# Where a chunk's normalised activations are transposed: TensorE and ScalarE in place of VectorE and DRAM, in a kernel with a written-out instruction order

## The chip, the cores and the metric

One core of a Trainium2 chip runs the whole kernel. The metric is device time in microseconds, the median of several executions. Engines: TensorE (PE, with its weight loads PEld), VectorE (DVE), ScalarE (ACT), GpSimd (POOL), and SyncE (SP), which here only issues DMAs.

## What is computed

A gated linear-attention recurrence over 768 steps, then one layer-norm and two-layer MLP with a residual.

```python
# q, k, v, alpha: (batch 4, heads 8, seq 768, dim 48), float32
for t in range(S):
    state = alpha[:, :, t, :, None] * state + einsum('bhd,bhe->bhde', k[:, :, t], v[:, :, t])
    y[:, :, t] = einsum('bhd,bhde->bhe', q[:, :, t], state)
x = y.transpose(0, 2, 1, 3).reshape(B, S, H * D)           # (4, 768, 384)
xn = (x - mean(x)) / sqrt(var(x) + 1e-6) * g_ln
out = x + maximum(xn @ w_ch1, 0) @ w_ch2                   # w_ch1 384 x 1536, w_ch2 1536 x 384
```

The two weights come as 64-bit floats; the kernel turns them into 32-bit ones itself.

## The kernel before

The sequence is cut into 6 chunks of 128 steps (c = 0 to 5). With 4 batches that makes 24 attention steps, each written as a Python generator (`attention`), which yields after every few instructions. Its stages: the logarithm of alpha and its running sum on PE (`lps`), two exponentials, the scaled q and k (L323, L325), their transposes (`kT`, `qT`: on PE for chunks 0 and 1, L351, and with VectorE's 32 x 32 transposes and a round trip over DRAM, `tr` and `td`, from chunk 2 on, L362 to L377), the scores (`aps`, L393 or L401), the causal mask (L407, L413), the state update (`sums`, L428, L437 to L443), the outputs (`yps`, L454 or L459 and L463), and the layer norm to `xn` (L466 to L515). The plain `x` goes to DRAM (`kept`) and comes back later as the residual (`ob`, L545).

Then `xn` (128 steps x 384) must be turned so that the 384 lie on the partitions (`xT`). There are two ways, chosen by `c < X_BY_DMA` at L519. In the first, PE makes three transposes into one PSUM bank (`xps`, L522) and VectorE (chunk 0) or ScalarE (later chunks) copies them out (L524). In the second, VectorE transposes in 32 x 32 blocks (`xr`, L528), SP issues four stores of 48 KB (`xd`, L532) and one load that puts the blocks in their places (L535). Before, chunks 0 to 3 take the first way and chunks 4 and 5 the second.

The MLP of chunk 0 runs straight (`hidden`, L558; `project`, L570). Chunks 1 to 5 use a scheme with fewer multiplications: a matrix product of 3 x 3 by 3 x 2 blocks is made of 15 products of sums of blocks (`hidden_product`, L848, in two halves r), and the second layer of 20 products (`product`, L674). The sums of weight blocks are made once on VectorE (`combine_first`, L800; `combine_weights`, L634), those of x and of the hidden values per chunk (`combine_x`, L825; `combine_hidden`, L661). Each product's result is added to the right places by VectorE, ScalarE and POOL (L690 to L740, L856 to L891), and the hidden values pass a Relu (L898). The weights arrive in 12 pieces and are rounded by VectorE and ScalarE (L215 to L232).

PSUM has 8 banks here: two for `sums`, and six that everything else shares (`tag="bank"`). Each engine runs its instructions in the order in which they were issued; an instruction that waits holds up what is behind it on its engine. The order is not left to a scheduler. It is a string of some 1,500 letters, `ORDER`; each letter takes the generator of that name one step further. Lower-case letters a to x are the 24 attention steps (c = 4 is q to t, c = 5 is u to x), A to L the weight pieces, Y and Z the first layer of chunk 0, P and Q its second layer, S and W the weight sums, X and N the sums of x and of hidden values, 1 and 2 the hidden products, R and U the Relus, M the second products, and O the residual loads.

Of the kernel before, what the change touches and what calls it, by code (L numbers as in the profile page):

```python
# [18 lines left out]
EPS = 1e-6  # L19
STAGED = 3  # L20
BY_DMA = 2
X_BY_DMA = 4
SPLIT = 4
AHEAD = 2
G = 32
# [5 lines left out]


ORDER = (
    "bacabcadaacbcaadbcadabcababbebaccbadbaaBbccaedcbceAeeaaacbfecfBcdafddeaedbdeafae"
    "bcdccbfgadhAdcgCcdbebeebfhggdfgbfffbCdcgfgecdfchgdfhgabcddchdhAiiegjhacehedhhjfg"
    "biAdfidAeBhBijffYYiCjZZYYifZYlZCgjYDlYYjjZZYBZYgDieEgDgDjZZekEhZYGZgZigZGeeYgYgg"
    "fZYEhfGfkChihiYFYijfgEhgkhFZYhgYfghijgkFeZZlGZShfZYHlhHfYFYZeZHelYiZgllPmZkJIgJk"
    "PeiYjJIflHeSZIQgkIlYSjiPkffennSQlOKjLSnSjmSQhKnSjLnKPkiljnhSQnLkkjkWknkShOmPhkhl"
    "kOOhWlmmphmQmkmXjWQnXjlSQjPmkilXSXkP2OXWjXQjkjW2iXoSWX2oWX22Pi2mnol1j1mom2omSpoo"
    "l1XSpk2oW2m112p1m2pm11m1W211pp12O122r22jnn21lpnmnjSml1riOn2l12Rl111kqS1m21W1Rkp2"  # L40
    "o21mUXpq1mU2rUrnmj1rl2Rno2oomqonrormpokO1rNM2Mipin1op1ionoqUM2qp2W12RkMmNqiMoRtk"
    "UrpkqNM1NoMliMlNUMMNMNMKNqMlNorMWrnmtltNRMsqppMWNMriMMMpNlsqqqnoqttNttMtMsXMMssM"
    "sMNMNMX1oXXppMvstM2MXMMNMsppXoMXoqMsMMXM1nqqv11Xq1trMq2tqX21rn12v1r2ur2r222rvsqs"
    "svsu1rs1nuvvt2s11ss11p22rtsvosn2uropuXru222221uts212stnU1211u1121222Op1Rp2tRU21R"
    "Us1pXqU11x2tO2MM1vwMUM12xuRvu1vurNNNNwtOuuMwRxvNtxRNutwwMM2MOwNXwMNuXMMtNM1rMMMw"
    "qtXMMMxNUNxtMMsNMMMxXxMtXtrMMqMNrMXNvutMMwNuMMMNMMMxMLMOM11vvuq2X2O2wMus1wX11222"
    "2r2Xt1222w22utsqxvw2x2ww1vx21sX12121xwvq2O2x2w111u1uvU121w12s1wuRvx12U11J1q21R1U"
    "OvRxU121wMMu2xxsRNMw2NNMRM1MUNN2MMuUMqXN1MrNNRMNvMXNXMMMM2MMMxNM1uNXMMNMNMOXMXMv"
    "MMXOMMMXxNxwxMMvNMMMMMXMx21w1x222212v12w222x122w2212X11UX2212121121121wx111MU11X"
    "2RR2v1211212211R1URU211XOUM2XNRX1MX1RM2MXN2MXNXNMXXMXMMMN111U1MN1M1122MNM1MM2MM1"  # L50
    "11NNN121O11NM1MM21N1112N1122M1MMM12MM12N222M22M2RM1M2N22MM2MU1ON2M22M2UURR22RNNM"
    "MNM1MMOMRMNMUUM2ONMNNNMO2MMMUMNMMMMMRMMNNMMMNMNMMNMMMMMMMMNMNMMMMMMM"
)


# [1 line left out]
def kernel(  # L57
# [236 lines left out]
    def attention(c, b):  # L294
# [222 lines left out]
        if c not in xT_of:  # L517
            xT_of[c] = work.tile([P, NF, B, P], FP32, name="xT", tag="xT")
        if c < X_BY_DMA:  # L519
            xps = ps.tile([P, NF, P], FP32, name="xps", tag="bank", bufs=6)  # L520
# [439 lines left out]
```

## Time and profile before

| | us |
|---|---|
| median of 3 runs | 421.02 (420.24 to 422.59) |
| the profiled execution | 420.14 |
| its span, first to last instruction | 418.3 |
| last matmul ends (from the span's start) | 415.15 |

The page's chain of work that ended last gives 89% of the span to PE, 4% to VectorE, 2% to DMA. Its costliest lines:

```profile
PE 89%; DVE 4%; DMA 2%; ACT 2%; issue 1%; POOL 0%; POOLq 0%; SPq 0%; DVEq 0%
PE hps L848 31%; PE ops L674 30%; PE ops L570 8%; PE hps L558 7%; PE aps L401 3%; PE yps L459 2%; PE yps L463 2%; PE sums L428 2%; DMA vn<-in_v_dram 2%; PE xps L522 1%; PE aps L393 1%; DMA ra<-in_alpha_dram 1%; PE lps L313 1%; DVE w L217 1%; PE tps L351 1%
```

The hidden products and the second products are 61% of the chain; `xps` is 1%. An fp32 matmul stands in the trace as two PE instructions, a transpose as one. A group's mean duration on PE is from start to modelled end; matmuls overlap, so what one costs on the path is read from start to start.

### The profile page before, as it was taken

To read this page: it belongs to the slowest core of one execution; us is meant where nothing else is said; L and a number is where in the kernel's file an instruction comes from. 1 tells how busy PE (TensorE), PEld (TensorE's weight loads), DVE (VectorE), ACT (ScalarE), POOL (GpSimd) and SP (SyncE) were. 2 spreads that over 40 slices of the span, in tenths; PEclk is the share of its full clock that TensorE was granted. 3 is DMA by queue.
4 is the path that set the end of the run, shared out by engine and by line. 5 is a ranking of instruction groups with operands and counts; after the bars stand their busy time and mean duration, and the time that the engine had idled before them with its cause. 6 is when DMAs were issued, how large, how long until landed. Compare 5 with 4: busy or idle time off the path is not lost.

```text
span 418.3 us, 11560 instructions
## 1 busy us (share of the span) xinstructions
PE 409.8 (98%) x4608; PEld 361.3 (86%) x4608; DVE 351.4 (84%) x713; ACT 177.5 (42%) x440; POOL 151.6 (36%) x164
## 2 busy tenths in 40 slices
PE   7998999999999999999999999999999999999996
PEld 5787888766578889998889999889998899999996
DVE  4999999999999989996888995688876767977873
ACT  5598447724243496414546603364313242014110
POOL 1011000003203980043395033493152940499123
PEclk9999999999999999999999999999999999999999
DMA  8999999987888778587684546433035200001201
GB/s 278 340 302 288 235 196 306 270 184 195 193 233 175 207 153 193 123 203 179 135 213 85 130 102 162 88 96 78 0 116 102 67 0 2 1 19 40 94 20 56
DMA packets 135037, 61.26 MB, mean 146 GB/s; under 512 B 90908, under 2 KB 131100, under 8 KB 134984
## 3 DMA queue, kind: packets, MB, share of 16 engines
q1 hardware_dynamic: 134440, 60.37, 56.1%
q8 instruction: 36, 0.59, 0.6%
q10 hardware_dynamic: 544, 0.17, 0.2%
q14 instruction: 17, 0.14, 0.1%
HBM read 43.12 MB, written 17.39 MB: 145 GB/s over the span
## 4 chain that ended last, share of the span: by engine, by line
PE 89%; DVE 4%; DMA 2%; ACT 2%; issue 1%; POOL 0%; POOLq 0%; SPq 0%; DVEq 0%
PE hps L848 31%; PE ops L674 30%; PE ops L570 8%; PE hps L558 7%; PE aps L401 3%; PE yps L459 2%; PE yps L463 2%; PE sums L428 2%; DMA vn<-in_v_dram 2%; PE xps L522 1%; PE aps L393 1%; DMA ra<-in_alpha_dram 1%; PE lps L313 1%; DVE w L217 1%; PE tps L351 1%
## 5 line engine op out<-in xcount | busy, mean ns | idle before, releaser
L690 POOL TENSOR_TENSOR ob<-ob,u 128x192 f32<-128x192 f32 x40 | 26.2, 665 | 64.5 <-DVE ob L687 48.3
L848 PE MATMUL hps<-sum,w 128*128 128x256 f32 x192 | 46.3, 381 | 0.0
L898 ACT ACTIVATE hT<-hT 128x512 f32<-128x512 f32 x48 | 28.7, 622 | 35.0 <-POOL hT L870 18.5
L443 POOL TENSOR_TENSOR mid<-mid,gate 112x192 f32<-112x192 f32 x20 | 11.6, 580 | 81.8 <-DVE mid L441 51.3
L674 PE MATMUL ops<-w,hT 128*128 128x192 f32 x224 | 40.5, 327 | 0.0
L848 PEld LDWEIGHTS hps<-sum,w 128*128 128x128 f32 x192 | 36.1, 190 | 5.0
L674 PEld LDWEIGHTS ops<-w,hT 128*128 128x128 f32 x224 | 37.1, 190 | 0.7 <-issue 0.2
L848 PE MATMUL hps<-xT,w 128*128 128x256 f32 x136 | 34.0, 380 | 0.0
L570 PE MATMUL ops<-w,hT 128*128 128x384 f32 x96 | 33.0, 492 | 0.0
L558 PE MATMUL hps<-xT,w 128*128 128x256 f32 x144 | 32.5, 382 | 0.0
L558 PEld LDWEIGHTS hps<-xT,w 128*128 128x128 f32 x144 | 27.0, 190 | 4.2
L674 PE MATMUL ops<-ws,sum 128*128 128x192 f32 x160 | 28.7, 327 | 0.0
L848 PEld LDWEIGHTS hps<-xT,w 128*128 128x128 f32 x136 | 25.5, 190 | 3.1
L570 PEld LDWEIGHTS ops<-w,hT 128*128 128x128 f32 x96 | 17.5, 190 | 10.8 <-DVE w L232 0.4
L674 PEld LDWEIGHTS ops<-ws,sum 128*128 128x128 f32 x160 | 26.5, 190 | 0.3
L684 DVE TENSOR_TENSOR ob<-ops,ob 128x192 f32<-128x192 f32 x50 | 17.2, 351 | 10.6 <-PE ops L674 6.5
L443 POOL TENSOR_TENSOR st<-st,gate 112x192 f32<-112x192 f32 x16 | 11.6, 725 | 35.6 <-DVE st L441 25.9
L674 PE MATMUL ops<-ws,hT 128*128 128x192 f32 x128 | 23.6, 328 | 0.0
L459 PEld LDWEIGHTS yps<-st,qT 48*64 48x64 f32 x320 | 19.9, 134 | 4.0 <-issue 2.3
L463 PE MATMUL yps<-vx,at 64*64 64x48 f32 x320 | 22.7, 219 | 0.0
L401 PEld LDWEIGHTS aps<-qT,kT 48*64 48x64 f32 x576 | 19.1, 134 | 4.1 <-issue 0.8
L459 PE MATMUL yps<-st,qT 48*64 48x48 f32 x320 | 22.0, 220 | 0.6 <-ACT x L486 0.6
(248 smaller groups left out, 1131.6 us busy)
## 6 DMA issues: line engine op xcount, KB each, us to landing
ws<-in_moe_w_ch_dram SPq DMA_DIRECT2D x12, 768.0 KB, 5.8
td<-tr SPq DMA_DIRECT2D x64, 96.0 KB, 2.8
vn<-in_v_dram SPq DMA_DIRECT2D x12, 384.0 KB, 6.9
kept<-x SPq DMA_DIRECT2D x24, 192.0 KB, 3.0
ob<-kept SPq DMA_DIRECT2D x24, 192.0 KB, 3.0
out_dram<-ob SPq DMA_DIRECT2D x19, 192.0 KB, 1.9
ra<-in_alpha_dram SPq DMA_DIRECT2D x16, 192.0 KB, 2.6
kT<-td SPq DMA_DIRECT2D x32, 96.0 KB, 3.4
```

Source lines behind the costliest of these rows:

```text
L401: nc.tensor.matmul(to, kT[rs, p, s], qT[rs, p, s], start=True, stop=True)
L428: nc.tensor.matmul(up[h, p], qk_of(c, b)[ts, 1, p, i, :h.stop - h.start], vn[ts, i, p], start=True, stop=True)
L443: nc.gpsimd.tensor_mul(new, new, by)
L459: nc.tensor.matmul(yps[i][halves[s], i, p], qT[rs, p, s], (now, mid)[s][rs, p], start=True, stop=r != i)
L463: nc.tensor.matmul(yps[r][halves[s], i, p], at[halves[r], p, s], by, start=r != i, stop=True)
L558: nc.tensor.matmul(hps, w1[:, j // 2, f, j % 2 * P:][:, :P], xT_of[0][:, f, bs], start=(f == 0), stop=(f == NF - 1))
L570: nc.tensor.matmul(ops_of[b], hT_of[c][:, j, b], w2[:, j], start=(j == 0), stop=(j == NJ - 1))
L674: nc.tensor.matmul(acc, lhs[:, j], rhs[:, j], start=(j == 0), stop=(j == NT - 1))
L684: nc.vector.tensor_add(x, acc, x)
L690: getattr(nc.gpsimd, f"tensor_{op}")(x, x, y)
L848: nc.tensor.matmul(acc[:, i], w, b, start=True, stop=True)
L898: nc.scalar.activation(out=x, in_=x, func=AFT.Relu)
```

## The change

One number and the string. Chunk 4 (attention steps q, r, s, t) now takes the first way at L519: three TensorE transposes and a ScalarE copy for each of its four batches, in place of one VectorE transpose, four stores and a load. Chunk 5 stays on the second way. These four steps have one yield less each, so the string has four letters less (1504 for 1508), and all of it was searched anew, so that nearly every engine's instructions stand in another order, from the first attention steps to the last products.

```diff
-X_BY_DMA = 4
+X_BY_DMA = 5
...
 ORDER = (
-    "bacabcadaacbcaadbcadabcababbebaccbadbaaBbccaedcbceAeeaaacbfecfBcdafddeaedbdeafae"
-    "bcdccbfgadhAdcgCcdbebeebfhggdfgbfffbCdcgfgecdfchgdfhgabcddchdhAiiegjhacehedhhjfg"
...
+    "abacabccadbbcacdbababbbbadaaaaccbadacbcecbaBccfaedeAeaaacefaecbfbcddddfbdeaafdcB"
+    "bdeaegdaceAchCbechbeeadcdgcbfcgcfbfgfcdfcgdbdddgCfehgfghhhbdegehdAibegdchefhigfd"
...
-    "11NNN121O11NM1MM21N1112N1122M1MMM12MM12N222M22M2RM1M2N22MM2MU1ON2M22M2UURR22RNNM"
-    "MNM1MMOMRMNMUUM2ONMNNNMO2MMMUMNMMMMMRMMNNMMMNMNMMNMMMMMMMMNMNMMMMMMM"
+    "M1MNMN1XM12MR11M1M1NM111M222R2M22MMMMMMNMN12N222MM2M2M2MM11U222RM222UMRUOMOMMMM2"
+    "ONMNN2MURUO22NMMNNMNUMMMNMMMMMMRMMMNNNMMMMNNMNMMMMMNMNMMMMMMMMMM"
```

More of the change, by code (lines that the diff above doesn't have):

```diff
@@ L33 @@
 ORDER = (
-    "bacabcadaacbcaadbcadabcababbebaccbadbaaBbccaedcbceAeeaaacbfecfBcdafddeaedbdeafae"
-    "bcdccbfgadhAdcgCcdbebeebfhggdfgbfffbCdcgfgecdfchgdfhgabcddchdhAiiegjhacehedhhjfg"
[L36 to L50, printed above, removed]
-    "11NNN121O11NM1MM21N1112N1122M1MMM12MM12N222M22M2RM1M2N22MM2MU1ON2M22M2UURR22RNNM"
@@ L52 @@
-    "MNM1MMOMRMNMUUM2ONMNNNMO2MMMUMNMMMMMRMMNNMMMNMNMMNMMMMMMMMNMNMMMMMMM"
+    "abacabccadbbcacdbababbbbadaaaaccbadacbcecbaBccfaedeAeaaacefaecbfbcddddfbdeaafdcB"
+    "bdeaegdaceAchCbechbeeadcdgcbfcgcfbfgfcdfcgdbdddgCfehgfghhhbdegehdAibegdchefhigfd"
+    "jjhhAAZgaBiBZjCBjijgZZiifYZiCYZifZYfDjegYeYlgejgDZYDYkYDYEZZlZYjgZfghhEGYfhgCZge"
+    "GEigYFfYZZYjhfhGkgYZijFZYZFYESYYkfYHhgiYHZlkfFigifgjhHZGleShgYShlZQeikefllklgZfn"
+    "YhSgJSjIHJQOIJekIflnfZPKeYekPSSQKOiiKZSljmjIQhlPnknjSnSnLLPnjOLkmSkknhOikkhShkkm"
@@ new lines @@
+    "WPjhllQmmmhmSWmPkhXQXWXnWPijXjQmiXSXjoX1S11lOP12l1op2QWXkmiSko2lW1jWmX2o2oooo2qW"
+    "2X22pmWmn12jqpSpl1p11j2p1m2pm12122pr22mmji2Okr1n211Ojninmlk1m2n21R21knU2lX1211Rl"
+    "U2W2pUm11npjr1krolpooRoUrnmonMnojrkor1irok221o1MplRnWiqpqRqoqqmUoNM1MNMMMqNNMkpi"
+    "1lMrNpRM2ltMNiolMpWMOs2qniMMpNmktlMopNroNMrWMrNUMNlqtMNnqqqsttoqtMqttMvJsMMMNNLM"
+    "MsmXossMMMMpmNNsqvmMpoMXMMXtMMmsMq1MnMqqXrtX2XXr11121r22X2Xq221ts12X2pvvv1u11r1p"
+    "rrs21ssuspsvpp1vuqt2srs2r2t1vOsuutu2s12t1121R2x12ouXnouO2r2x1r1tun112O1Uw2RnnR22"
@@ new lines @@
+    "p1Usw222UMpsMM11qM22tMv1Nut2UMN1UONuuRRNtMtNXwMMMUtXNwNsvuvxNM1wXNMxRtxNsx1MMxs2"
+    "MNqrMNMMMMMuMMwMuMNwNrMMxvMvuMXXMMwMXMNMMqqNMxXMuMMvu21X11r21v22Xus2212u12wsu1M2"
+    "22X21wO1wwxwv2x2Owq21w1uOt21x211qrrX1t222u122vUwx12Uxv1wwxs1t2112RROU1112x2RMMUM"
+    "sw1NMRt112tXxNNUXMXNRXv1KMMM1MNMMMwNMXNNRNx2NMMvUuMNxwMMXxMMMxuM12MvMNvNXxOMMMNv"
+    "MMMvNwNMMMMMxwMMMXXM2x1112vxw112Mx1111w1XX112O211222122211221122R1222122U1O2w21U"
+    "122vXR1RU1uR222MMM21X1MU1XMNX2N1RXXXNXMUMXM1O2NMX12NN12NMU1M11122111RN111N211NM1"
```

## The prediction

> **What bounds the kernel now.** I read the page's busy line first, then the same busy times by stretches, then what TensorE (PE) waited for, then the chain of waits, then single groups and the stretch around two tight places.
>
> ```profile
> PE 409.8 (98%) x4608; PEld 361.3 (86%) x4608; DVE 351.4 (84%) x713; ACT 177.5 (42%) x440; POOL 151.6 (36%) x164
> ```
>
> A share over the whole span hides where an engine is the limit, so the stretches come next. Columns: the stretch, its length, then busy time and (instructions) of PE, PE's weight loads, VectorE (DVE), ScalarE (ACT) and GpSimd (POOL), granted clock, DMA share, GB/s.
>
> ```profile
> 0.00:38.76 38.76, 34.10 (x573) 27.99 (x573) 32.13 (x71) 28.08 (x72) 5.12 (x10) 1.00 0.97 303
> 38.76:115.00 76.24, 75.57 (x972) 57.01 (x968) 74.43 (x132) 37.16 (x89) 10.53 (x13) 1.00 0.90 228
> 115.00:200.00 85.00, 84.93 (x1330) 75.76 (x1333) 77.04 (x161) 41.47 (x109) 33.27 (x37) 1.00 0.76 183
> 200.00:300.00 100.00, 100.00 (x1123) 91.71 (x1116) 82.98 (x186) 46.48 (x123) 45.97 (x46) 1.00 0.49 111
> 300.00:410.00 110.00, 110.00 (x603) 104.01 (x602) 81.86 (x159) 24.04 (x49) 53.88 (x53) 1.00 0.16 44
> ```
>
> The first hidden matmul starts at 38.76. From there PE has 0.74 us without work up to 410, and its clock is granted in full: this is a PE-bound kernel after the start. Up to 115 us VectorE is as full (74.43 of 76.24): there the two bind together. Chunk 4's x, which the change moves, is worked on between 244 and 292 us, where PE has no idle time at all and VectorE has about a sixth.
>
> ```profile
> PE lps L313 <- ACT la L308: 1.6, 2, 1.4
> PE xps L522 <- DVE xn L511: 1.5, 1, 1.5
> PE yps L459 <- ACT x L486: 0.6, 1, 0.6
> ```
>
> Columns: us in total, times, longest. The first two are of the start (before 34 us); the third is the only one left later, at 114 us. PE never waits for x's way over DRAM (xr, xd). So shortening that way can't shorten the run, and work given to PE adds to it.
>
> **The change, part by part.** The rows (line, engine, operation, count, busy us, mean ns):
>
> ```profile
> L522 PE MATMUL xps<-consts,xn 128*128 128x128 f32 x48 | 7.8, 278 | 1.5 <-DVE xn L511 1.5
> L528 DVE STREAM_TRANSPOSE xr<-xn 128x384 f32<-128x384 f32 x8 | 4.5, 568 | 0.0
> L524 ACT COPY xT<-xps 128x384 f32<-128x384 f32 x12 | 5.4, 471 | 6.8 <-PE xps L522 6.8
> ```
>
> Added: for chunk 4's 4 batches, 3 TensorE transposes and one ScalarE copy each (48 transposes become 60, 12 copies become 16). The mean of 278 ns is not the price: matmuls overlap, and the chain of waits shows what three take on the path.
>
> ```profile
> 160.89 0.33 PE xps L522 x3
> 161.22 1.30 PE ops L674 x8
> 162.52 0.33 PE xps L522 x3
> ...
> 167.80 0.48 PE xps L522 x3
> ```
>
> 0.33 us between matmuls, 0.48 right behind the small attention matmuls. Chunk 4's four groups now stand among hidden products and second products (none behind attention matmuls), so 4 x 0.33 = 1.3 us, at most 4 x 0.48 = 1.9. With no idle time on PE in that stretch all of it is path: +1.3. The Trainium skill ("TensorE: Matmul & The Clock Gate", Wait — 56ns, not 53.3ns?) has 55.6 ns from start to start of matmuls 128 wide, by which 12 would cost 0.7 us as an estimate and the sum below be 1.2; the rows here have 0.33 / 3 = 110 ns for these fp32 transposes, so the measurement decides.
>
> The 4 copies (4 x 0.47 = 1.9 us) lie on ScalarE, busy 46.48 of 100 us there: cover enough; what their waits hold up is a rival below.
>
> Removed: 4 VectorE transposes (4 x 0.57 = 2.3 us), and on SP's queue 16 stores xd and 4 loads xT. VectorE has idle time from 200 us on and PE waits for none of these: worth 0. SP's later issues (kept, gate, ob) come a little earlier; PE's waits name none of them.
>
> Moved: the order of nearly everything. I counted both programs by engine. The work ahead of PE's first hidden matmul is the same set on PE (64 transposes of q and k, 12 of x, 72 of scores and running sums, and so on) and on VectorE the same 69 rows' work, so only waits can move that point. Two places differ.
>
> First, the start. VectorE is the chain from about 8 to 38 us. Before, it does a product of the second pair of batches between the first two q/k products and the copies out of PE:
>
> ```profile
> 9.94 0.56 DVE L323 TENSOR_TENSOR qk<-rk,lps 128x384 f32<-128x384 f32 x1
> 10.55 0.69 DVE L356 COPY kT<-tps 112x512 f32<-112x512 f32 x1
> 11.16 0.55 DVE L325 TENSOR_TENSOR qk<-rq,more 128x384 f32<-128x384 f32 x1
> 11.63 0.68 DVE L356 COPY kT<-tps 112x512 f32<-112x512 f32 x1
> ```
>
> After, both copies stand ahead of these products. The 16 transposes that they read run from 9.48 to 11.39, so the second copy can end no sooner than 11.39 + 0.69 = 12.1, against 12.3 before, and two products (2 x 0.46 us from start to start) are still owed: 0.7 us later. VectorE's next waits (0.42 us for the next transposes at 15.7, 0.26 at 18.0) can swallow nearly all of that. Bounds 0 to 0.7; I take 0.35.
>
> Second, the last piece of w2. PE's projection of chunk 0 starts on it in the same nanosecond as VectorE finishes it:
>
> ```profile
> 101.96 0.96 DVE L232 SCALAR_TENSOR_TENSOR w<-w,ws 128x768 f32<-128x768 f32 x1
> 102.92 2.23 PEld L570 LDWEIGHTS ops<-w,hT 128*128 128x128 f32 x8
> ```
>
> In the new order VectorE has 12 instead of 11 of the weight sums of L800 ahead of that piece and otherwise the same, while PE's work up to there is equal: one L800 of 128x512 is 0.70 us (its group's mean 703 ns, 0.62 from start to start), so PE starts about 0.65 us later, unless VectorE's idle time is cut: between 38.76 and 115 it has 76.24 - 74.43 = 1.8 us. Bounds -1.2 (all of it gone) to +0.65. The first w2 pieces get more room, and for every product of chunks 1 to 5 I compared VectorE's summed work up to the sum that it reads with PE's summed work up to it: the smallest margin goes from 0.2 to about 0.6 us, so no new wait there, with a margin too thin to be sure. For idle time regained at all these places I take -0.4.
>
> Sum: 1.3 + 0.35 + 0.65 - 0.4 = +1.9 us. The end is alike (17 second products in a row before, 18 after; 3.2 us from the last matmul's end at 415.15 to the span's end). The profiled execution took 420.14 us (span 418.3 and 1.8 around it), 0.9 under the median of 421.02; 420.14 + 1.9 = 422.0, and the same on the median gives **422.9 us**, +0.45%.
>
> **The rivals.** (1) ScalarE's queue becomes a wait. In the new order two copies L524 stand one behind the other, of transposes that lie 8 hidden-product matmuls apart on PE (8 x 0.43 = 3.5 us), and behind them the copy out (L474) of an attention output that PE had finished before both. ScalarE works in order, so this output's two PSUM banks of six stay taken some 3.9 us longer, with the transposes' own bank besides; the next products then have three banks and their own ScalarE copies (L856, L864) queue behind. Price: up to 3.5 us of PE's time if nothing else can be issued, so 422.9 + 3.5 = 426.4. For it: the wait at 114 us is of just this kind (PE behind L486, 0.6 us, when four banks are out). Against: ScalarE is half idle, and three banks rotate. It decides from about one product's delay (0.9 us) on.
>
> (2) Not slower: the new order takes up VectorE's 1.8 us of idle time before 115 us and the 0.6 us wait at 114. Then 1.3 - 1.2 - 0.6 = -0.5: 420.5. For it: VectorE is full there and nothing on PE forces its waits. To be faster by 0.5% it would have to regain 3.4 us, more than all PE idle time after the start.
>
> (3) The path of chunk 4's x did bind, and VectorE with it: then 2.3 us come off and 1.3 go on, 420.0. The Trainium skill ("VectorE: DVE Perf Modes", Rules for kernel authors) says so: a 128x128 transpose belongs on TensorE where PSUM can take it, and plain strided DMAs are a trap. Against: 110.00 busy of 110.00 on PE, and the first hidden product of chunk 4 starts at 295.6 without a wait.
>
> **How the numbers follow.** Half a per cent (2.1 us) is about what a measurement of this kernel can tell from no change, since the three runs spread over 2.35 us. Chances: my forecast's mechanism 0.52, centred on 422.9, where its terms can vary by 1.5 us either way (half of it below the 423.1 that is +0.5%); rival 1 0.25, nearly all slower; rival 2 0.16 and rival 3 0.07, with a third of these faster by over 0.5%. So slower 0.26 + 0.22 = 0.48, faster 0.07, same 0.45. The range goes from rival 2's 420.5 to rival 1's 426.4, rounded to 420.4 and 426.4; the forecast's own is 421.4 to 424.4.
>
> **What would show it.** Right: PE busy time up by about 1.3 us; L522 x60 with 0.33 us per three on the chain between 260 and 285 us; the first hidden matmul at 38.8 to 39.5 us; the last piece of w2 at 103.3 to 104; PE idle only at the same places. Wrong: PE idle between 260 and 300 us released by ScalarE (rival 1), a first hidden matmul before 38.3 us or the third wait gone (rival 2), or a run shorter although PE does more (rival 3). A stall of PE over 1 us anywhere from 40 to 410 us that I don't name would make the sum wrong.

## The result and the profile after

The changed kernel took 425.32 us (median of 6 runs, 424.45 to 427.22) against 420.69 for before on the same chip (6 runs, 420.12 to 422.59). The ratio is 1.011, with a 95% interval of 1.0084 to 1.0135: slower by 4.6 us, where 1.9 were forecast. The profiled execution took 425.47 us and its span is 423.7, 5.4 more than before's.

The busy line of the page after, and from the groups of lines the three that the change touches (mean ns of one after the comma, then the idle time before them):

```profile
PE 413.3 (98%) x4620; PEld 362.5 (86%) x4620; DVE 352.6 (83%) x709; ACT 180.6 (43%) x444; POOL 148.5 (35%) x164
L522 PE MATMUL xps<-consts,xn 128*128 128x128 f32 x60 | 10.0, 276 | 0.5 <-DVE xn L511 0.5
L524 ACT COPY xT<-xps 128x384 f32<-128x384 f32 x16 | 7.5, 467 | 11.1 <-PE xps L522 11.1
L528 DVE STREAM_TRANSPOSE xr<-xn 128x384 f32<-128x384 f32 x4 | 2.2, 558 | 0.0
```

The change does what it says: 12 transposes more on TensorE, 4 copies more on ScalarE, 4 transposes fewer on VectorE. PE's busy time rose by 3.5 us, far more than the 1.3 us that the forecast gives 12 transposes.

The same stretches as before, except that the first one ends at 40.00, where the first hidden matmul now starts (38.8 before):

```profile
0.00:40.00 40.00, 34.53 (x572) 27.91 (x572) 32.07 (x70) 27.95 (x72) 5.48 (x10) 1.00 0.90 288
40.00:115.00 75.00, 74.87 (x915) 56.28 (x912) 73.36 (x129) 35.54 (x85) 7.04 (x12) 1.00 0.93 233
115.00:200.00 85.00, 83.53 (x1293) 73.98 (x1286) 75.85 (x158) 41.12 (x105) 31.98 (x37) 1.00 0.74 179
200.00:300.00 100.00, 99.80 (x1200) 90.69 (x1199) 80.96 (x175) 45.47 (x116) 47.35 (x47) 1.00 0.41 97
300.00:410.00 110.00, 110.00 (x599) 103.43 (x598) 84.28 (x168) 30.21 (x66) 49.93 (x49) 1.00 0.17 46
```

PE's idle time up to 115 us has shrunk (0.13 of 75.00, against 0.67 of 76.24). New is the third stretch: 1.47 us idle between 115 and 200 us, where before had 0.07. From the first hidden matmul to the end of the span it is 383.7 us now (423.7 - 40.0) and was 379.5 (418.3 - 38.8). That makes 1.2 us lost at the start and 4.2 behind it. Of the 4.2, 1.3 are the added transposes. PE's idle time explains only another 1.1 (1.80 from 40 to 410 us, against 0.74), so the rest must lie in time that counts as busy. That the modelled ends of matmuls cover short stalls is my reading of this; no view shows it directly. The distance between two fixed events is the safer measure, and the table below uses it.

What PE itself waited for (us in total, times, longest):

```profile
PE aps L401 <- ACT kT L356: 1.9, 1, 1.9
...
PE hps L848 <- ACT x L486: 0.5, 1, 0.5
PE hps L848 <- DVE u L885: 0.5, 2, 0.3
...
PE ops L674 <- ACT x L486: 0.4, 1, 0.4
```

The releaser is now ScalarE: once at the start (L356) and twice later by L486, the copy of an attention output out of PSUM. The wait for L486 that before had at 114 us is gone. What ScalarE did at the two later places (start, duration, in brackets the idle time ahead and what ended it):

```profile
142.45 1.15 ACT L898 ACTIVATE hT<-hT 128x512 f32<-128x512 f32 x2 [2.18 <-POOL hT L870]
143.51 0.47 ACT L486 ACTIVATE x<-yps 128x384 f32<-128x384 f32 x1
...
178.67 0.52 ACT L308 ACTIVATE la<-ra 128x384 f32<-128x384 f32 x1 [3.12 <-DMA ra<-in_alpha_dram]
...
180.71 0.47 ACT L486 ACTIVATE x<-yps 128x384 f32<-128x384 f32 x1
```

Both times ScalarE stands still, for GpSimd or for a load, at an instruction that PE does not need yet, and the copy that gives PE two PSUM banks back is behind it in the queue. Neither stall is long (0.53 us without work at 143 us, 0.42 at 181): no stall over 1 us stands in this trace between 40 and 410 us. The stall at the start is of the same kind. The chain of waits there, in order of time (start, duration, what):

```profile
9.38 5.94 DMA row<-eq
...
15.33 2.19 DMA gate<-row
...
18.79 6.68 DMA ra<-in_alpha_dram
...
25.49 0.52 ACT la L308
26.02 0.48 ACT kT L356
```

A 2 KB store (`row`) is issued behind the three chunk 1 loads and takes 5.94 us. The load that reads it back waits for it on SP's queue, so the later alpha load is issued at 18.79 (17.20 before), and ScalarE's logarithm waits for that with the copy of kT, which PE needs, behind it.

### The profile page after: what moved, and what is told of

Read it like the earlier page. It is cut to its first block, busy times and chain, and to the rows that moved or that the text cites. A ratio compares the mean times of both kernels' runs of the same rounds, so it can differ in the third digit from the quotient of the medians.

```text
span 423.7 us, 11548 instructions
## 1 busy us (share of the span) xinstructions
PE 413.3 (98%) x4620; PEld 362.5 (86%) x4620; DVE 352.6 (83%) x709; ACT 180.6 (43%) x444; POOL 148.5 (35%) x164
## 4 chain that ended last, share of the span: by engine, by line
PE 86%; DMA 6%; DVE 3%; ACT 2%; issue 1%; POOL 1%; SPq 0%; DVEq 0%
PE ops L674 30%; PE hps L848 29%; PE hps L558 8%; PE ops L570 7%; PE aps L401 3%; DMA ra<-in_alpha_dram 3%; PE yps L459 2%; PE yps L463 2%; PE sums L428 2%; DMA row<-eq 1%; PE xps L522 1%; DMA vn<-in_v_dram 1%; PE lps L403 1%; POOL hT L870 1%; PE tps L351 1%
## 5 line engine op out<-in xcount | busy, mean ns | idle before, releaser
L690 POOL TENSOR_TENSOR ob<-ob,u 128x192 f32<-128x192 f32 x40 | 27.5, 697 | 61.6 <-DVE ob L687 47.6
L570 PEld LDWEIGHTS ops<-w,hT 128*128 128x128 f32 x96 | 17.8, 190 | 10.7
L401 PEld LDWEIGHTS aps<-qT,kT 48*64 48x64 f32 x576 | 19.1, 134 | 5.7 <-issue 2.6
L401 PE MATMUL aps<-qT,kT 48*64 48x64 f32 x576 | 22.0, 222 | 2.0 <-ACT kT L356 1.9
L463 PE MATMUL yps<-vn,at 64*64 64x48 f32 x320 | 22.1, 220 | 0.0
```

The costliest lines, as they stand in the source:

```text
L401: nc.tensor.matmul(to, kT[rs, p, s], qT[rs, p, s], start=True, stop=True)
L463: nc.tensor.matmul(yps[r][halves[s], i, p], at[halves[r], p, s], by, start=r != i, stop=True)
L570: nc.tensor.matmul(ops_of[b], hT_of[c][:, j, b], w2[:, j], start=(j == 0), stop=(j == NJ - 1))
L690: getattr(nc.gpsimd, f"tensor_{op}")(x, x, y)
```

## The experiments

All were timed beside runs of before on the same chip. "Rest" is the span less the start of the first hidden matmul, in the profiled execution, which is one execution and not always a typical one (2.2 us above the median in x4_new_order, 2.3 in x3_store_near). The string of before is the old order, that of the changed kernel the new one. "x3", "x4", "x5", "x6" say how many chunks are transposed on TensorE.

| kernel | median us | before, same chip | ratio, 95% | first hidden matmul | rest |
|---|---|---|---|---|---|
| before | 420.69 | | | 38.8 | 379.5 |
| the changed kernel | 425.32 | 420.69 | 1.0084 to 1.0135 | 40.0 | 383.7 |
| x5_old_order | 427.00 | 420.62 | 1.0123 to 1.0171 | 38.8 | 386.1 |
| x4_new_order | 430.17 | 420.62 | 1.0203 to 1.0260 | 40.1 | 390.5 |
| x5_old_copy_near | 421.64 | 420.42 | 1.0011 to 1.0049 | 38.6 | 380.6 |
| x6_new_order | 427.13 | 420.42 | 1.0131 to 1.0210 | 39.8 | 384.5 |
| new_row_first | 424.67 | 420.62 | 1.0066 to 1.0113 | 39.6 | 383.2 |
| new_v1_later | 426.34 | 420.62 | 1.0109 to 1.0165 | 41.0 | 383.1 |
| new_copy_first | 424.24 | 420.42 | 1.0059 to 1.0109 | 39.6 | 382.1 |
| new_four_moves | 423.48 | 420.42 | 1.0042 to 1.0094 | 39.4 | 383.1 |
| new_two_moves | 422.77 | 420.68 | 1.0041 to 1.0083 | 38.9 | 383.7 |
| new_three_moves | 423.08 | 421.15 | 1.0038 to 1.0064 | 38.8 | 382.0 |
| x4_row_late | 423.32 | 420.97 | 1.0042 to 1.0090 | 41.7 | 379.3 |
| x3_old | 430.93 | 420.68 | 1.0222 to 1.0262 | 39.7 | 388.3 |
| x3_mno_old | 428.21 | 420.68 | 1.0160 to 1.0210 | 39.1 | 387.2 |
| x3_store_near | 431.42 | 421.15 | 1.0227 to 1.0261 | 40.2 | 391.7 |
| x3_mno_store_near | 429.47 | 421.15 | 1.0190 to 1.0240 | 39.9 | 387.8 |
| x3_mn | 425.11 | 420.97 | 1.0073 to 1.0120 | 39.6 | 384.2 |

**The number and the string apart.** The change has two halves, so each was run with the other's old value.

```diff
# x5_old_order: before with
-X_BY_DMA = 4
+X_BY_DMA = 5
# x4_new_order: the changed kernel with
-X_BY_DMA = 5
+X_BY_DMA = 4
# and one letter more for each of q, r, s, t, behind its 27th
```

> The order string of before, with chunk 4's x on TensorE and ScalarE (each of the four steps then does nothing at its last letter). Theory A (the transposes cost 0.33 us per three on PE, the rest of the loss comes from the new order): 420.7 + 1.3 = 422.0 us, ratio 1.003, L522 x60. Theory B (the transposes and copies of chunk 4 themselves make the loss, through banks and ScalarE's queue): near 425.3, ratio 1.011.

> The new order string, with chunk 4's x on VectorE and DRAM as before (each of the four steps gets its missing letter behind its last one). Theory A: 425.3 - 1.3 = 424.0 us, ratio 1.008 to before. Theory B: near 420.7. If chunk 4's load now lands too late for its sums, up to 2 us more than A.

By the medians both are worse than the changed kernel. In x4_new_order chunk 4's x lands too late for an order that was made for the short way. PE's waits, and the VectorE instruction behind the longest:

```profile
PE ops L674 <- DVE ob L684: 4.5, 1, 4.5
PE ops L674 <- ACT x L486: 2.2, 1, 2.2
```

```profile
298.25 0.43 DVE L825 TENSOR_TENSOR sum<-xT 128x256 f32<-128x256 f32 x1 [5.34 <-DMA xT<-xd]
```

A sum of x blocks waits 5.34 us for the load, and VectorE's next work on PE's results stands behind it. The second wait, 2.2 us for L486, is the one at 178 us again. Behind the 4.5 us stall PE's granted clock stands at 0.50 from 302.5 to 305.5 us (PE has 10 instructions from 303 to 305.5, and 17 from 306 to 308.5 at a clock of 1.00), by estimate another 1.2 us, and all six executions have a mean clock of 0.991 to 0.996, where before has 1.000 or 0.999. So neither half can be priced with the other's order. A fair price of the transposes needs an order that suits them, with nothing else moved.

**What spoils x5_old_order, and the price of the transposes.** In x5_old_order the copy stands where the stores to DRAM stood, 31 to 49 letters behind the transposes. Its transposes and copies for chunk 4 (min/median/max ns, then first and last start):

```profile
L522 PE MATMUL xps<-consts,xn x12: 272/273/329, 245.2 to 278.1; 128*128 128x128 f32 x12
...
L524 ACT COPY xT<-xps x4: 459/471/493, 263.0 to 284.2; 128x384 f32<-128x384 f32 x4
...
248.00:264.00 16.00, 12.83 (x92) 10.35 (x92) 5.81 (x18) 3.99 (x11) 3.90 (x7) 1.00 0.48 126
```

The first transposes are at 245.2 and the first copy only at 263.0: banks stay taken for 18 us, and PE is busy for 12.83 of the 16 us between. The next kernel moves the four copies alone.

```diff
# x5_old_copy_near: x5_old_order with the copy letters of q, r, s, t
-  31 to 49 letters behind their transposes
+  7 or 8 letters behind their transposes
```

> The order of before with chunk 4's x on TensorE, as in x5_old_order, but each of the four copies that free the bank stands 6 letters behind its transposes instead of 29 to 49. Theory (the transposes cost their 1.3 us of TensorE, and what x5_old_order lost beyond that were banks held too long): the five stalls of 0.6 to 1 us between 248 and 258 us are gone, time 420.6 + 1.3 = 421.9 (421.4 to 422.6), below the changed kernel's 425.3. Rival (ScalarE's added copies themselves are late, whatever the order): stalls stay, 424.5 or more. Rival (the transposes are free, because TensorE is not the bound there): 420.6.

```profile
L522 PE MATMUL xps<-consts,xn x12: 272/273/328, 244.7 to 272.4; 128*128 128x128 f32 x12
...
L524 ACT COPY xT<-xps x4: 478/479/488, 245.2 to 272.7; 128x384 f32<-128x384 f32 x4
...
248.00:264.00 16.00, 16.00 (x123) 14.44 (x123) 9.05 (x23) 5.61 (x14) 3.59 (x7) 1.00 0.53 138
```

The same views of this kernel: each copy follows at once, PE is busy for all 16 us, and the time is 421.64 instead of 427.00 with the same instructions. This is chunk 4 on TensorE with hardly anything else moved, and it costs 0.3% (0.1 to 0.5%), 1.3 us with an interval of 0.5 to 2.1; the rest of its span is 1.1 us longer than before's. The term for the transposes agrees with this. If they cost the same in the new order, the changed kernel's other 3.3 us belong to that order.

**A second dose.**

```diff
# x6_new_order: the changed kernel with
-X_BY_DMA = 5
+X_BY_DMA = 6
```

> The changed kernel with chunk 5's x on TensorE and ScalarE as well; no letter is moved (the third x letter of chunk 5 does nothing). A second dose of the same change, without a new order. Theory (the dose costs TensorE's 12 transposes, 1.3 us, and the rest of the change's loss is the order's): 425.3 + 1.3 = 426.6 (426.0 to 427.2). Rival (each dose costs the whole 4.6 us, by ScalarE or by banks): 429 to 430. Rival (chunk 5's way over DRAM binds): below 425.3.

427.13, 1.8 us above the changed kernel by the medians. The intervals of the two overlap, so the size is loose, but a dose that costs the whole 4.6 us is not what this shows. Three of its six executions have a mean granted clock of 0.995 or 0.996 (427.0 to 431.2 us), the three others took 426.1 to 427.3. The waits of the new order (ScalarE's L356 at the start, L486 at 143 us) are there again unchanged.

**The waits of the new order, one by one.** The edits move single letters (a7 is the seventh a of the string, counted from 1):

```diff
# new_row_first: the row store (a7) ahead of the chunk 1 loads (b6)
-  c d b a b a b b b b
+  c d b a a b b b b b
# new_copy_first: the copy L486 (l19) ahead of the two Relus at 142 us
-  n 2 1 R 2 1 k n U 2 l X
+  n 2 1 l R 2 1 k n U 2 X
# new_v1_later: the chunk 5 logarithm (v1) behind the copy p19
-  t t M v J s ... M M M M p m N N
+  t t M J s ... M M M M p v m N N
# new_four_moves: these three, and the chunk 1 logarithm (g1) behind the copy of kT (e10)
-  b d e a e g d a c e A c h
+  b d e a e d a c e g A c h
# new_two_moves: new_row_first and new_copy_first
# new_three_moves: new_two_moves and new_v1_later
```

> The changed kernel with two neighbouring letters swapped, so that SP issues the 2 KB store row of batch 0 (chunk 0) ahead of the three loads of chunk 1 instead of behind them. Theory A1 (that store lands late behind 1.2 MB of loads, the gate load that needs it holds SP for 3.5 us, so weights and chunk 1's second alpha come late, ScalarE waits 3.0 us for alpha and PE 2.1 us behind it): SP's stop at 12 us shrinks below 1.5 us, the first hidden matmul starts near 38.8 instead of 40.0, total 0.5 to 1.3 us less: 424.0 to 424.8. Rival: the wait moves to the next transfer and the total stays within 0.3 us.

> The changed kernel with one letter moved: the logarithm of chunk 5's batch 1 (L308) behind the copy L486 of chunk 3's batch 3 on ScalarE instead of ahead of it. Theory A2 (ScalarE waits 3.1 us for that alpha at 178 us and holds two PSUM banks behind it, PE waits 0.6 us at 180): PE's wait at 180 us goes, total 0.5 us less. Rival (VectorE or the other drains are late too): the wait stays or moves by a product, total unchanged.

> The changed kernel with the single move at 142 us: the copy that frees two PSUM banks stands ahead of the two Relus that wait 2.2 us for GpSimd. Theory (the wait in ScalarE's queue makes TensorE's stall of 0.70 us at 143 us and the lost time stays): 425.3 - 0.7 to -1.4 = 424.2. Rival (it is regained by the next wait anyway): 425.3.

> The changed kernel with four moves of letters that the profile names: the row store ahead of the chunk 1 loads (a7 before b6), the logarithm that waits 3.0 us for its load behind the copy of kT (g1 after e10), the copy out of PSUM ahead of the two Relus that wait for GpSimd at 142 us (l19 before the sixteenth-letter pair R1), and the chunk 5 logarithm that waits 3.1 us at 178 us behind the copy p19. Theory (the loss beyond 1.3 us is in these waits of the new order): -0.65 (measured for the first move alone), -0.7 to -1.4 at 143 us, -0.5 to -1.0 at 180 us, 0 to -0.5 for the second at the start: 425.3 - 2.5 = 422.8 (421.9 to 423.7). Rival (a wait that is taken away comes back later, since the same operands have to pass): 424.7, as with the first move alone.

> The changed kernel with the two moves that helped alone: the row store ahead of the chunk 1 loads (424.67 alone) and the copy ahead of the Relus at 142 us (424.24 alone); the changed kernel has 425.32. Theory (both losses are separate and stay lost): -0.65 and -1.1 add up, 423.6 (423.1 to 424.1), and the stall of 1.1 us that new_four_moves has at 151 us, which comes from moving the two logarithms, is not there. Rival (they overlap): 424.2 or more.

> new_two_moves (422.77) and the chunk 5 logarithm behind the copy p19 as well: it waits 3.1 us for its load, and TensorE stands 1.82 us at 178 us in the profile of new_two_moves. Theory (the loss of the changed kernel is the transposes and three waits of its order): 422.8 - 1.0 to -1.8 = 421.6 (421.0 to 422.2), which is before plus the 1.3 us of the transposes, within what is measured. Rival (something else of the new order costs as well, the wait comes back later): 422.5 or more.

new_copy_first came as the theory said: 424.24. ScalarE's queue there, to be compared with the stall above:

```profile
140.54 0.49 ACT L486 ACTIVATE x<-yps 128x384 f32<-128x384 f32 x1 [0.59 <-PE yps L459]
142.14 1.15 ACT L898 ACTIVATE hT<-hT 128x512 f32<-128x512 f32 x2 [1.11 <-POOL hT L870]
```

The copy now runs at 140.54 rather than 143.51, the Relus wait for GpSimd as before, PE has no wait for L486 left, and the rest of the span is 1.6 us shorter. new_row_first came to 424.67. The interval of each of the two overlaps with the changed kernel's, so the sizes of the single moves (1.1 and 0.65 us) are loose. SP's gate load, which waits for the row store, in the changed kernel and in new_two_moves, which has the same move:

```profile
12.18 3.53 SPq L419 DMA_DIRECT2D gate<-row  x2
```

```profile
12.28 0.92 SPq L419 DMA_DIRECT2D gate<-row  x2
```

The two issues take 0.92 instead of 3.53 us. In all five profiles with the new order's start they take 3.4 to 3.5 us and the first hidden matmul is at 39.6 to 41.0; with the store moved they take 0.9 to 1.4 us and it is at 38.8 to 39.6 (four profiles). Both moves together took off 2.5 us by the medians (2.0 by the ratios, whose intervals just part), down to 422.77.

new_v1_later is a miss: the stall at 180 us is gone from its trace, but the time, 426.34, is no better, and its start came 1 us later with the same instructions. The clock has a part in that start. The page's row of the granted clock (40 slices of 10.6 us, in tenths):

```profile
PEclk9989999999999999999999999999999999999999
```

Behind the 2.0 us wait for kT at 25 us the clock stands at 0.50 from 28.6 to 32.0 us, with PE busy throughout: by estimate, at half the clock, 1.7 us. In the changed kernel nearly the same wait (1.9 us) is followed by a clock of 1.00. Four of new_v1_later's six executions have a mean clock of 0.995 or 0.996 and none of the changed kernel's has; but the other two took 426.0 and 426.7, so the clock alone does not make the miss. Nor did new_three_moves better new_two_moves: the ratios, 1.0051 and 1.0062, are not to be told apart. That this wait holds PE is seen in the profile of new_two_moves, on ScalarE and on PE:

```profile
177.61 0.53 ACT L308 ACTIVATE la<-ra 128x384 f32<-128x384 f32 x1 [4.41 <-DMA ra<-in_alpha_dram]
```

```profile
PE ops L674 <- ACT x L486: 1.7, 1, 1.7
```

The logarithm waits 4.41 us for its load there, 3.12 in the changed kernel and 2.34 in new_row_first, so the price of this place differs from one execution to the next. The profiled execution of new_two_moves took 424.39, which is 1.6 above its median. new_four_moves, with g1 moved besides, was no better than new_two_moves: its trace has a new PE stall of 0.9 us at 151 us, whose cause stays open.

**The start's trait alone, in the kernel before.**

```diff
# x4_row_late: before, with b4, b5, c6 and b6 drawn ahead of a7
-  a a d b c a d a b c a b
+  a d b c d b c b a a a a
```

> Before, with nothing of the change but one trait of the new order at the start: batch 0's row store of chunk 0 stands behind the three chunk 1 loads (b6 ahead of a7, the letters b4, b5 and c6 drawn ahead with it), as in the changed kernel. The x of chunk 4 keeps its way over DRAM. Theory (a small store issued behind three large loads lands late, SP waits for it at the gate load, and the chunk 1 loads and the logarithm behind them come late): SP waits 3 to 4 us at the gate load and the first hidden product starts 0.5 to 1.3 us later, 420.7 + 0.65 = 421.3 (420.9 to 422.2). Rival (the late start comes from something else of the new order): 420.6.

423.32, more than either theory gave. The rest of the span, 379.3, is before's to 0.2 us, so the whole loss is in the start: the first hidden matmul is at 41.7. What SP's queue waited for in the first 22 us (us in total, times, longest):

```profile
SPq L419 <- DMA row<-eq: 3.9, 1, 3.9
SPq L330 <- ACT eq L320: 2.2, 1, 2.2
```

The wait at the gate load for the row store is there as foretold, 3.9 us against 1.7 in before and 4.1 in the changed kernel. But the test is less clean than meant: with the letters drawn ahead VectorE's products shift too, both row stores start later (the first at 9.15, against 7.25 before), and PE waits 1.4 us for a product (`PE tps L351 <- DVE qk L325`). So the mechanism is shown, and the size for the store alone is better read from new_row_first.

**The other direction.** If a transpose costs PE 0.11 us, before would gain by giving up more of them.

```diff
# x3_old: before, with chunk 3's x over DRAM; loads placed 16 to 22 letters behind the stores, X23 later
-X_BY_DMA = 4
+X_BY_DMA = 3
# x3_mno_old: as x3_old, the last batch left on TensorE, X23 not moved
-        if c < X_BY_DMA:
+        if c < 3 or (c, b) == (3, 3):
# x3_store_near, x3_mno_store_near: the same two, stores 6 letters behind VectorE's transposes
# x3_mn: only batches 0 and 1 of chunk 3 over DRAM, stores near
+        if c < 3 or (c == 3 and b > 1):
```

> The change turned the other way: the order of before with chunk 3's x too over VectorE's transposes and DRAM (X_BY_DMA = 3), so that TensorE transposes 36 blocks instead of 48. Its four loads of xT stand 16 to 20 letters behind their stores, and the first combining letter of chunk 3's x (X23) is moved some 50 letters back, behind the last of these loads. Theory (a transpose on TensorE costs its 0.11 us wherever TensorE is the bound, and VectorE and the DMA queues have room): 420.5 - 1.3 = 419.2 (418.7 to 420.0). Rival (chunk 3's data comes too late over DRAM, as chunk 4's did in x4_new_order): 422 or more. Rival (VectorE's four added transposes of 0.57 us bind): 421 to 423.

> As x3_old, but the last batch of chunk 3 stays on TensorE, and no combining letter is moved: nine transposes fewer than before. Theory: 420.5 - 1.0 = 419.5 (419.0 to 420.2). Rival (late data or VectorE): 421 or more.

> x3_old again (chunk 3's x over DRAM too, 12 transposes fewer than before), with the stores to DRAM 6 letters behind VectorE's transposes instead of 11 to 44, so that the buffer of the transposed row comes free early. In x3_old and x3_mno_old VectorE's next such transpose waits 6.2 us for this buffer, and TensorE 4.3 to 4.5 us for what stands behind it on VectorE. Theory (this wait was the loss there, a transpose costs TensorE 0.11 us): 420.6 - 1.3 = 419.3 (418.8 to 420.0). Rival (the way over DRAM is too late for chunk 3 whatever the order, at its last batch above all): 422 or more.

> As x3_store_near, with the last batch of chunk 3 left on TensorE and no combining letter moved. Theory: 420.6 - 1.0 = 419.6 (419.0 to 420.2). Rival: 421 or more.

> Only batches 0 and 1 of chunk 3 go over DRAM besides chunks 4 and 5 (six transposes fewer than before), stores 6 letters behind VectorE's transposes. In x3_mno_store_near two such transposes stood next to each other and the second waited 6.3 us for the row buffer of the first, whose stores waited in SP's queue. Theory (that wait was the loss, and it needs two of them together): no stall at 211 us, 420.7 - 0.65 = 420.0 (419.6 to 420.9). Rival (one such transpose alone loses as much as it saves, for it holds a row buffer until its four stores have landed): 421 to 423.

All five are misses: 425.11 to 431.42. The waits of x3_mno_store_near between 205 and 218 us:

```profile
DVE xr L528 <- DMA xd<-xr: 6.3, 1, 6.3
PEld hps L848 <- DVE qk L323: 4.7, 1, 4.7
PE hps L848 <- DVE qk L323: 4.3, 1, 4.3
```

VectorE's second transpose waits 6.3 us until the stores of an earlier one have left the row buffer. These stores stand on SP's queue behind loads of v and are issued at 211.7, though the transpose was done at 209. Moving their letters nearer did not help, because SP was late, not the letter. PE waits 4.3 us for what is behind that transpose on VectorE. The stall is not all that it costs. The clock row of this page (slices of 10.7 us):

```profile
PEclk9999999999999999999969999999999999999999
```

The granted clock stands at 0.50 from 214.5 to 221 us; for 4.6 us of that PE works, at half its pace (11 instructions from 217 to 221, and 22 from 222 to 226 at a clock of 1.00), so by estimate some 2 us go there. Every execution of the four x3 kernels other than x3_mn has a mean clock of 0.988 to 0.996 (before beside them: 0.996 to 1.000, mostly 1.000), which over 430 us is 1.7 to 5.2 us of clock withheld, some of it while PE stood still anyway. x3_mn, where the two do not meet, has no such stall, and a clock of 0.999 or 1.000, but its rest is still 4.7 us longer than before's, with some 0.65 us less work on PE (six transposes at 0.11). ScalarE once waits for a row buffer there:

```profile
161.66 0.49 ACT L486 ACTIVATE x<-yps 128x384 f32<-128x384 f32 x1 [3.22 <-DVE xr L528]
```

and PE waits at 175 and 227 us for loads of qT (`PE aps L401 <- DMA qT<-td`, 0.3 and 1.0 us in total), which stand on SP behind the five added DMA issues of each batch. From 161 to 227 us SP's issues take 58 of the 66 us, 48 in before. So at this place the way over DRAM cost more than the transposes that it saved; that SP's fuller queue is the reason for all of it is likely, but no run separates it.

No version was found that beats before. x5_old_copy_near is 3.7 us faster than the changed kernel with the same way for x, by the medians.

## Why the prediction came out as it did

The side was right and the size was not: +4.6 us against +1.9. Step by step:

- **The transposes, +1.3: right.** On the chain of waits of the changed kernel they are where the forecast had them:

```profile
271.03 0.33 PE xps L522 x3
...
274.82 0.33 PE xps L522 x3
...
281.12 0.33 PE xps L522 x3
```

  The fourth group, at 289.69, takes 0.33 us as well. x5_old_copy_near prices them at 1.3 us by the time of the whole kernel. The Trainium skill ("TensorE: Matmul & The Clock Gate", Wait — 56ns, not 53.3ns?), by whose 55.6 ns they would cost 0.7 as an estimate, falls inside that run's interval too; it is the rows, 110 ns each again, that speak against it. (The sum by that figure would have been 1.3, not the 1.2 of the forecast.)
- **"PE busy time up by about 1.3 us" was a bad test.** It rose by 3.5 in the changed kernel and by 0.7 in x5_old_copy_near, with the same instructions.
- **The start, +0.35: mis-sized, for a reason that the forecast left out.** I counted VectorE's products, its chain before. The first hidden matmul came 1.2 us later in the two profiles, because of SP and ScalarE: the row store behind the loads, the gate load's 3.53 us on SP, the logarithm's 3.0 us on ScalarE ahead of kT's copy. I had seen that the loads and the store changed places and gave SP's queue no price. By time, moving the row store back is worth about 0.65 us (new_row_first, with an interval that overlaps the changed kernel's); two profiles say more than is there, since starts with the same instructions spread widely (last section).
- **The last piece of w2, +0.65: there, but not kept.** It runs at 103.58, 1.62 later than before, 1.2 of which is the later start. PE's idle time from 40 to 115 us fell instead, 0.13 against 0.67, and the wait at 114 us is gone, as rival 2 had it.
- **Idle time regained, -0.4: the step that failed.** It rested on "no new wait there", a comparison of VectorE's summed work with PE's for every product of chunks 1 to 5. The margins of VectorE held. The new waits came through ScalarE's queue and PSUM banks, which that comparison does not contain: at 143 us (1.1 us by new_copy_first) and at 178 us (seen in traces, not resolved in time). What I forecast as a small gain of 0.4 was a loss of some 2 to 3 us (4.6 less the transposes and the start); of this the runs place about 1.1 at 143 us, and where the rest lies stays open.
- **Rival 1 had the mechanism at the wrong place.** An in-order ScalarE with a waiting instruction ahead of a copy that frees banks is what happened, but not through the added copies, and not at 260 to 300 us: there PE was idle for 0.2 us in all, though two of the copies L524 waited 4.8 us for PE.
- **Rival 3, and the Trainium skill ("VectorE: DVE Perf Modes", Rules for kernel authors):** for chunk 4 the way over VectorE and DRAM bound nothing, since x5_old_copy_near, which takes it away, is slower than before. For chunk 3 the time goes the way that the Trainium skill has it: five kernels that put its x on the strided DMAs lost 4 to 10 us. But what their traces show is SP's queue, the row buffer and the clock behind the stalls; that the strided transfers themselves were slow no run here shows.

The sum of what was measured, from the ratios: 4.6 us, of which 1.3 are the transposes, 2.0 the two waits at the start and at 143 us (new_two_moves still loses 2.6), and perhaps 0.5 the one at 178 us (new_three_moves still loses 2.1, with an interval of 1.6 to 2.7). Some 0.8 us remains between new_three_moves and x5_old_copy_near. It is no more than their intervals allow, and no run here says where it lies. That the side came out right is partly luck: of the four terms the first alone held, and one of the others had the wrong sign.

## What to carry to other kernels

When an order changes, check for every engine that works in order, and for the DMA-issuing queue, which instruction that waits now stands ahead of one that frees a shared buffer; margins of the busiest engine alone miss this. To price one moved step, keep the order and move only that step's own letters, so that its buffer is held briefly. A path that is "hidden anyway" at one place of a kernel can bind at another, where its queue or its buffers are full. When a stall of the busiest engine is priced, look at its granted clock behind the stall too.

## What the runs showed of the hardware that was not expected

- A 2 KB store to DRAM issued 0.5 us behind the last of three loads of 384 KB took 5.94 us to land.
- The start of eight kernels whose instructions are the same up to the first hidden matmul (before, and the x5 and x3 kernels of the old order) put that matmul anywhere from 38.6 to 40.2 us (38.6 to 39.9 without x3_store_near, where the granted clock is 0.50 from 36 to 39 us). Differences of 1 us at a start where the DMA engines are 97% busy can't be read from one pair of profiles.
- The same 4620 PE instructions gave 410.5 to 414.7 us of PE busy time in nine kernels, in another ranking than the times (x5_old_order has 412.4 and is the slowest of them): PE's modelled busy time is no measure of its work.
- After a stall of PE the granted clock stood at 0.50 for 3 us and more in several profiles: from 302.5 to 305.5 us behind 4.5 us of waiting in x4_new_order, from 214.5 to 221 in x3_mno_store_near, from 28.6 to 32.0 behind 2.0 us in new_v1_later. Behind 1.9 us at the same place in the changed kernel it stayed at 1.00. So a stall can cost more than its own length, and not in every execution.
